# Wo as two partial sums in column mode, a new unit order, and the last rows kept on chip, in a recurrent-memory transformer kernel

## Chip, cores, metric

The kernel runs on one core of a Trainium2 chip. The metric is the device time of one execution in microseconds (us). Every time below comes from runs that the results mark as fast. "Before" is the tuned kernel the change starts from, "after" the changed one. Engines: PE (TensorE matmul), PEld (its weight loads), DVE (VectorE), ACT (ScalarE), POOL (GpSimd), SP (DMA issue).

## The reference, cut to what matters

```python
def _A_ref(x, mem0, Wq, Wk, Wv, Wo, seg_len):      # S=2048, Dm=512, H=32, Dh=128, M=8, seg=32
    mem = mem0
    for s in range(64):                            # strictly one after the other
        h = concat([mem, x[:, 32*s:32*s+32]])      # 8 memory rows + 32 rows
        q, k, v = h @ Wq, h @ Wk, h @ Wv           # 512 -> 32 heads x 128
        p = softmax(mask(q k^T / sqrt(128)))
        o = (p v) @ Wo                             # 4096 -> 512
        mem = o[:, :8]                             # the next segment needs these 8 rows
        outs.append(o[:, 8:])
# B: linear/dot attention over 4 blocks of 512 rows, 32 heads of 16; result = g*a + (1-g)*b
```

Branch A is a chain of 64 segments: the first 8 rows of a segment's Wo result are the memory of the next. Branch B depends on nothing in A, and the kernel uses its pieces to fill waits.

## The kernel before

A segment is a list of *units*. Each engine executes its part of the units in the order of this list. (The code of this section is condensed.)

```python
A_ORDER = """
    bS K0 Q0 K1 Q1 TK0 TQ0 TK1 V0 bP TQ1 bP bT S0 Fc M0 S1 N0 V1 M1 PV0 E0a N1 E0b Ff PV1 W0 E1a E1b bS W1 Fc bS bP WT
    Ff bT Ff""".split()
A_ENG = dict(K0="dve", K1="act", Q0="dve", Q1="act", V0="act", V1="dve", TK0="act", TK1="dve",
             TQ0="dve", TQ1="act", E0a="act", E0b="act", E1a="dve", E1b="act", last=1)
```

K, Q, V are the projections (0 and 1: halves of 16 heads); T their transposes; S scores; M the softmax sums; N the normalising on DVE; PV the product with V; E its evictions from PSUM; W the two halves of Wo; WT the transposition of Wo's result, from which DVE copies the memory rows into `hT` for the next segment. bS, bP, bT are scores, product and late pieces of branch B. Fc and Ff take the next *fill* piece: a projection pass for the next group of four segments (or a left-over Wo pass) for Fc, and a transposing piece or a piece of a finished group's output ("tail") for Ff. "Left rows" in the text are the last 8 rows of each segment, which a group projects together.

Projections, scores, sums and Wo run in *column mode*: the array is used as four tiles of 128 rows by 32 columns, `128*32` in the timelines below. Transposes and the B product are `128*128` there, PV and the B scores `32*128`.

```python
def wo(b):                      # 2 x 16 matmuls of 512 columns
    ...
    for i in range(4):
        for j in range(4):
            h = 16 * b + 4 * j + i
            pe.matmul(pb[bk][32*j:32*(j+1), :], OT_sb[:, h, 0:32], Wo_sb[:, h, :], ...)
    ...
    if b == 1:                  # high part on ACT, the rest on DVE, each in two pieces of 256 columns
        for k in range(2): evac("act", aW_sb[:, 0, cs], pb[bk][:, cs], ...)
        for k in range(2): dve.tensor_tensor(aW_sb[:, 1, cs], pb[bk][:, cs], aW_sb[:, 0, cs], subtract)

def w_t():                      # 8 matmuls in 128x128 mode: transpose and add the four row groups
    for k2 in range(2):
        for c in (2 * k2, 2 * k2 + 1):
            for k in range(2):
                pe.matmul(pb[bk][:, 32*c:32*(c+1)], aW_sb[:, k, 128*c:128*(c+1)], selL[:, :], ...)
    ...  # DVE: copy the memory rows to hT, the others to aT_st
```

At the end, groups 14 and 15 were finished one after the other, after the last segment, and their rows made a trip through HBM:

```python
for _, u in rest: u()
...
while tails < ngrp or late:
    next_tail(ngrp)
    late.pop(0)[1]()
```

The softmax here doesn't subtract the row's maximum and nothing guards it: scores larger than these inputs give would overflow.

Of the kernel before, what the change touches and what calls it, by code (L numbers as in the profile page):

```python
# [223 lines left out]
def build(nc, es, A_x, A_mem0, A_Wq, A_Wk, A_Wv, A_Wo, B_wq, B_wk, B_wv, B_wo, B_beta, gate_w, out, dbg=None):  # L224
# [31 lines left out]
    def alloc(stack, *specs):  # L256
        for name, shape, dt, n in specs:
# [8 lines left out]
          ("selL", [128, SEG], BF16, 0), ("onesb", [128, 128], BF16, 0), ("mneg", [128, 4, 224], BF16, 0),  # L266
# [18 lines left out]
          ("OT_sb", [128, H, L], BF16, 0), ("OTL", [128, H, SEG], BF16, 2), ("aW_sb", [128, 2, 512], BF16, 0),  # L285
# [82 lines left out]
def plan_const(v):  # L368
# [3 lines left out]
    ident, onesb, mneg, selL = v.ident, v.onesb, v.mneg, v.selL  # L372
# [24 lines left out]
    def late():  # L397
        rl, rob, rmk = Rs("selL"), Rs("onesb"), Rs("mneg")
        gp(lambda g: g.memset(selL[:], 0.0), rl, "selL0", True)
        gp(lambda g: g.memset(onesb[:], 0.0), rob, "onesb0", True)  # L400
# [239 lines left out]
class BAttn:  # L640
# [167 lines left out]
    def finish(self, sb, f):  # L808
# [3 lines left out]
        def ft(pe):  # L812
            ins = None
            for q in range(4):
# [11 lines left out]
    bS K0 Q0 K1 Q1 TK0 TQ0 TK1 V0 bP TQ1 bP bT S0 Fc M0 S1 N0 V1 M1 PV0 E0a N1 E0b Ff PV1 W0 E1a E1b bS W1 Fc bS bP WT  # L826
    Ff bT Ff""".split()
A_ENG = dict(K0="dve", K1="act", Q0="dve", Q1="act", V0="act", V1="dve", TK0="act", TK1="dve",
             TQ0="dve", TQ1="act", E0a="act", E0b="act", E1a="dve", E1b="act", last=1)


def plan_a(v, nseg):
# [10 lines left out]
    OT_sb, OTL, aW_sb, t1_sb, aT_st, selL, g_sb, omg_sb, out2d, g_out = (  # L843
        v.OT_sb, v.OTL, v.aW_sb, v.t1_sb, v.aT_st, v.selL, v.g_sb, v.omg_sb, v.out2d, v.g_out)
# [58 lines left out]
    def ol_units(g):  # L903
# [28 lines left out]
        def ut():  # L932
# [14 lines left out]
            B.give(bk)  # L947
            P.dma(P.group("as%d" % g, "as%d" % par), lambda sp: sp.dma_start(v.aTd[g], aT_st[par][:, :, :]),
# [4 lines left out]
    def tail_units(g):  # L953

        sb, q = g // 4, g % 4
        P.dma(P.group("og%d" % g, "og"), lambda sp: sp.dma_start(oTg[:, :, :], v.oTd[sb, :, :, 128 * q:128 * (q + 1)]),
              reads=[Rs("oTd%d_%d" % (sb, f)) for f in range(4)], writes=[Rs("oTg")], name="ldo%d" % g, scratch=True)
        P.dma(P.group("al%d" % g, "al"), lambda sp: sp.dma_start(aTg[:, :, :], v.aTd[g]), reads=[Rs("aTd%d" % g)], writes=[Rs("aTg")],
              name="lda%d" % g, scratch=True)
# [16 lines left out]
        def uf():  # L976
            bk = B.take()

            def f_atr(pe):
                ins = None  # L980
                for c in range(C):
                    ins = pe.transpose(pb16[bk][:, c * 128:(c + 1) * 128], aTg[:, c, :], ident[:, :])
                return ins
            P.op("pe", f_atr, reads=[Rs("aTg"), Rs("ident")], writes=[rbank[bk]], name="atr%d" % g)
# [11 lines left out]
    def segment(s, fill):  # L996
# [111 lines left out]
        def wo(b):  # L1108
            if b == 0:
                wb["bk"] = B.take()  # L1110
            bk = wb["bk"]

            def f(pe):
                ins = None
                for i in range(4):
                    for j in range(4):
                        h = 16 * b + 4 * j + i
                        ins = pe.matmul(pb[bk][SEG * j:SEG * (j + 1), :], OT_sb[:, h, 0:SEG], Wo_sb[:, h, :],  # L1118
                                        start=(b == 0 and i == 0), stop=(b == 1 and i == 3))
                return ins  # L1120
            P.op("pe", f, reads=[Rs("OT%d_%d" % (b, half)) for half in range(2)] + [Rs("Wo")], writes=[rbank[bk]], name="wo%d_%d" % (s, b))
            if b == 1:
                for k in range(2):
                    cs = slice(256 * k, 256 * (k + 1))
                    evac("act", aW_sb[:, 0, cs], pb[bk][:, cs], [bk], [Rs("aWh%d" % k)], "hi%d_%d" % (s, k))
                for k in range(2):
                    cs = slice(256 * k, 256 * (k + 1))
                    P.op("dve", lambda d, cs=cs: d.tensor_tensor(aW_sb[:, 1, cs], pb[bk][:, cs], aW_sb[:, 0, cs], ALU.subtract),  # L1128
                         reads=[rbank[bk], Rs("aWh%d" % k)], writes=[Rs("aWl%d" % k)], name="lo%d_%d" % (s, k))
                B.give(bk)  # L1130

        def w_t():
            bk = B.take()
            for k2 in range(2):
                def f(pe, k2=k2):
                    ins = None
                    for c in (2 * k2, 2 * k2 + 1):
                        for k in range(2):
                            ins = pe.matmul(pb[bk][:, SEG * c:SEG * (c + 1)], aW_sb[:, k, 128 * c:128 * (c + 1)], selL[:, :],  # L1139
                                            start=(k == 0), stop=(k == 1))  # L1140
                    return ins
                P.op("pe", f, reads=[Rs("aWh%d" % k2), Rs("aWl%d" % k2), Rs("selL")], writes=[rbank[bk]], name="aT%d_%d" % (s, k2))
            asrc = pb[bk][:, 0:128].rearrange("p (j t) -> p j t", t=SEG)
            if s + 1 < nseg:
                P.op("dve", lambda d: d.tensor_copy(hT[(s + 1) % 2][:, :, 0:M], asrc[:, :, 0:M]),  # L1145
                     reads=[rbank[bk]], writes=[Rs("hTm%d" % ((s + 1) % 2))], name="hm%d" % (s + 1))
            P.op("dve", lambda d: d.tensor_copy(aT_st[par][:, :, SEG * r:SEG * (r + 1) - M], asrc[:, :, M:SEG]),
# [51 lines left out]
    late, rest, tails = [], [], 0  # L1199

    def next_tail(done):

        nonlocal tails
        if tails < done and bat.jobs_done >= 4 * (tails // 4) + 4 and not late:
            late.extend(tail_units(tails))
            tails += 1
    for g in range(ngrp):
        fill = (left_units(g + 1) if g + 1 < ngrp else []) + rest
        for r in range(4):
            s = 4 * g + r  # L1210
            if s < nseg:
                next_tail(g - 1)
# [4 lines left out]
    for _, u in rest:  # L1217
        u()
    if nseg == 64:
# [6 lines left out]
        while tails < ngrp or late:  # L1226
# [35 lines left out]
```

## Time and profile before

| before | us |
|---|---|
| time, median of 3 (range) | 1118.8 (1115.9 to 1122.4) |
| profiled execution | 1122.7, span 1121.0 |
| start of segment 1 | 111.5 |
| segments 1 to 57, each (mean) | 15.81 |
| from the last WT to the end | 20.6 |

First, the page: busy time of the engines, and the chain that ended last by engine.

```profile
PE 1006.3 (90%) x24389; PEld 547.4 (49%) x24389; DVE 511.8 (46%) x1309; ACT 670.3 (60%) x1371; POOL 212.2 (19%) x544
PE 76%; ACT 9%; DVE 8%; DMA 3%; issue 3%; SPq 0%; POOL 0%; ACTq 0%; DVEq 0%; POOLq 0%
```

PE, with 76% of the chain, is the engine to look at; a faster ACT or DVE (9% and 8% of it) can help here only where PE waits for it. Next, the list of waits of PE (who waited for whom: total us, times, longest).

```profile
PE ps L1081 <- DVE Pn_sb L1071: 40.9, 46, 1.1
PE ps L967 <- DMA oTg<-scr_oTd: 8.3, 2, 4.3
PE ps L1139 <- DVE aW_sb L1128: 7.3, 12, 1.4
PE ps L939 <- DVE hT L1145: 6.7, 15, 0.7
PE ps L967 <- DVE V_sb L321: 5.5, 13, 0.5
```

L1081 is the second PV waiting for the normalised P, L1139 is WT waiting for the subtraction, L939 the transposition of left-over Wo rows, L967 the tail's B matmul. The wait of 9.0 us for the first left rows (startup) is left out. Now the PE timeline of one segment, from M1 to the next segment's first projection (start, length, engine, line, operation, what, shapes, count, idle before).

```profile
510.40 0.28 PE L1056 MATMUL ps<-P_sb,onesb 128*32 128x160 bf16 x8
510.61 0.27 PE L1081 MATMUL ps<-Pn_sb,V_sb 32*128 32x40 bf16 x16
...
511.91 0.28 PE L1081 MATMUL ps<-Pn_sb,V_sb 32*128 32x40 bf16 x16 [0.93 <-DVE Pn_sb L1071]
...
512.21 1.05 PE L1118 MATMUL ps<-Wo_sb,OT_sb 128*32 128x512 bf16 x16
513.19 0.39 PE L708 MATMUL ps<-QTj,KTj 32*128 32x256 bf16 x4
513.51 1.05 PE L1118 MATMUL ps<-Wo_sb,OT_sb 128*32 128x512 bf16 x16
514.38 1.04 PE L858 MATMUL ps<-Wv_sb,xL 128*32 128x512 bf16 x16
...
515.67 0.36 PE L755 MATMUL ps<-Vj,PT 128*128 128x17 bf16 x8
515.97 0.58 PE L1139 MATMUL ps<-selL,aW_sb 128*128 128x32 bf16 x8
516.40 0.28 PE L783 MATMUL ps<-MZj,pQj 128*128 128x68 bf16 x4
```

How to read it: the ends of pipelined matmuls are modelled and lengths overlap, so compare *starts*. Wo's second half starts at 513.51 and the next pass at 514.38: 0.87 us for 16 matmuls. WT starts at 515.97 and what follows at 516.40: 0.43. Where the array mode changes there is about 0.1 us more (512.21 to 513.19 is 0.98 for the same 16 matmuls). There is 0.93 us of nothing ahead of the second PV, and nothing at all between Wo and WT: the fill pass (514.38), B's scores and B's product cover eviction and subtraction. The last is the PE timeline of the end.

```profile
1100.34 0.58 PE L1139 MATMUL ps<-selL,aW_sb 128*128 128x32 bf16 x8 [1.37 <-DVE aW_sb L1128]
1100.85 1.91 PE L921 MATMUL ps<-Wo_sb,OTL 128*32 128x512 bf16 x32
...
1108.90 1.89 PE L967 MATMUL ps<-woB_sb,oTg 128*128 128x512 bf16 x4 [4.27 <-DMA oTg<-scr_oTd]
...
1115.27 1.89 PE L967 MATMUL ps<-woB_sb,oTg 128*128 128x512 bf16 x4 [4.06 <-DMA oTg<-scr_oTd]
```

Two tails in a row, each with over 4 us for its load, and their 4 matmuls at half clock (the clock record has 0.5 from 1106.4 to the end).

### The profile page before, as it was taken

To read this page: it belongs to the slowest core of one execution; us is meant where nothing else is said; L and a number is where in the kernel's file an instruction comes from. 1 tells how busy PE (TensorE), PEld (TensorE's weight loads), DVE (VectorE), ACT (ScalarE), POOL (GpSimd) and SP (SyncE) were. 2 spreads that over 40 slices of the span, in tenths; PEclk is the share of its full clock that TensorE was granted. 3 is DMA by queue.
4 is the path that set the end of the run, shared out by engine and by line. 5 is a ranking of instruction groups with operands and counts; after the bars stand their busy time and mean duration, and the time that the engine had idled before them with its cause. 6 is when DMAs were issued, how large, how long until landed. Compare 5 with 4: busy or idle time off the path is not lost.

```text
span 1121.0 us, 54313 instructions
## 1 busy us (share of the span) xinstructions
PE 1006.3 (90%) x24389; PEld 547.4 (49%) x24389; DVE 511.8 (46%) x1309; ACT 670.3 (60%) x1371; POOL 212.2 (19%) x544
## 2 busy tenths in 40 slices
PE   8968989999999999999999999999999999999874
PEld 4423545455554555454455554555455555454432
DVE  4743444444445444444454545444444545444331
ACT  4434666666666666666566666666666666655432
POOL 6100121211122121221221222211221122120000
PEclk9988999999999999999999999999999999999997
DMA  8895000000011010000111010000101010000001
GB/s 283 276 323 187 11 15 10 20 11 15 18 27 46 24 28 23 18 18 14 32 32 33 18 32 18 15 21 18 41 23 28 23 27 24 4 15 15 27 3 34
DMA packets 66176, 51.80 MB, mean 46 GB/s; under 512 B 34320, under 2 KB 64408, under 8 KB 64408
## 3 DMA queue, kind: packets, MB, share of 16 engines
q1 hardware_dynamic: 65944, 48.33, 14.7%
q8 instruction: 192, 3.15, 1.2%
q14 instruction: 40, 0.33, 0.1%
HBM read 33.60 MB, written 14.70 MB: 43 GB/s over the span
## 4 chain that ended last, share of the span: by engine, by line
PE 76%; ACT 9%; DVE 8%; DMA 3%; issue 3%; SPq 0%; POOL 0%; ACTq 0%; DVEq 0%; POOLq 0%
PE ps L858 37%; PE ps L1118 10%; PE ps L867 6%; PE ps L708 4%; ACT PT L716 3%; PE ps L755 3%; PE ps L584 2%; DVE Pn_sb L1067 2%; PE ps L921 2%; PE ps L967 2%; PE ps L1081 2%; PE ps L559 1%; PE ps L1139 1%; DMA scr_pQd<-stgp 1%; ACT R_sb L1060 1%
## 5 line engine op out<-in xcount | busy, mean ns | idle before, releaser
L716 ACT ACTIVATE PT<-ps 128x1024 bf16<-128x1024 f32 x160 | 163.1, 1022 | 59.7 <-PE ps L708 55.0
L1118 PE MATMUL ps<-Wo_sb,OT_sb 128*32 128x512 bf16 x2048 | 137.3, 391 | 3.3 <-DMA Wo_sb<-in_A_Wo_dram 3.3
L858 PE MATMUL ps<-Wv_sb,hT 128*32 128x512 bf16 x2048 | 134.6, 381 | 1.6 <-DVE amem L804 0.9
L858 PE MATMUL ps<-Wk_sb,hT 128*32 128x512 bf16 x2048 | 134.3, 382 | 0.8 <-DVE hT L1145 0.6
L724 POOL TENSOR_SCALAR_AFFINE_SELECT PT<-PT 128x256 bf16<-128x256 bf16 (+1 forms) x224 | 98.3, 439 | 191.6 <-ACT PT L716 182.6
L858 PE MATMUL ps<-Wq_sb,hT 128*32 128x512 bf16 x2048 | 133.6, 381 | 0.0
L1172 POOL COPY OTL<-OT_sb 128x256 bf16<-128x256 bf16 x64 | 25.4, 397 | 514.6 <-DVE OT_sb L321 394.0
L1128 DVE TENSOR_TENSOR aW_sb<-ps,aW_sb 128x256 bf16<-128x256 f32 x128 | 48.3, 419 | 157.2 <-ACT aW_sb L319 157.2
L319 ACT ACTIVATE KN_sb<-ps 128x512 bf16<-128x512 f32 x64 | 38.2, 597 | 117.2 <-PE ps L858 117.2
L319 ACT ACTIVATE OT_sb<-ps 128x320 bf16<-128x320 f32 x192 | 75.7, 428 | 19.2 <-PE ps L1090 18.9
L858 PEld LDWEIGHTS ps<-Wq_sb,hT 128*32 128x32 bf16 x2048 | 55.2, 97 | 56.1 <-issue 1.1
L1060 ACT ACTIVATE R_sb<-ps 128x160 f32<-128x160 f32 x128 | 38.8, 303 | 65.5 <-PE ps L1056 65.5
L858 PEld LDWEIGHTS ps<-Wk_sb,hT 128*32 128x32 bf16 x2048 | 49.2, 97 | 56.6 <-issue 7.1
L1081 PE MATMUL ps<-Pn_sb,V_sb 32*128 32x40 bf16 x2048 | 35.5, 178 | 44.2 <-DVE Pn_sb L1071 40.9
L321 DVE COPY QT_sb<-ps 128x512 bf16<-128x512 bf16 x64 | 27.2, 424 | 95.6 <-PE ps L867 95.6
L1118 PEld LDWEIGHTS ps<-Wo_sb,OT_sb 128*32 128x32 bf16 x2048 | 43.9, 97 | 49.7 <-issue 18.5
L321 DVE CAST KN_sb<-ps 128x512 bf16<-128x512 f32 x64 | 44.1, 689 | 51.4 <-PE ps L858 51.3
L1067 DVE TENSOR_TENSOR Pn_sb<-P_sb,R_sb 128x160 bf16<-128x160 bf16 x128 | 44.1, 344 | 47.7 <-ACT R_sb L1063 39.0
L755 PEld LDWEIGHTS ps<-Vj,PT 128*128 128x128 bf16 x1280 | 44.4, 96 | 41.7 <-issue 28.4
L708 PE MATMUL ps<-QTj,KTj 32*128 32x384 bf16 (+3 forms) x512 | 62.9, 303 | 1.1 <-ACT PT L716 0.2
L319 ACT ACTIVATE V_sb<-ps 128x512 bf16<-128x512 f32 x64 | 38.2, 597 | 42.8 <-PE ps L858 42.8
L858 PEld LDWEIGHTS ps<-Wv_sb,hT 128*32 128x32 bf16 x2048 | 46.0, 95 | 34.7 <-ACT R_sb L1060 1.5
(136 smaller groups left out, 1832.6 us busy)
## 6 DMA issues: line engine op xcount, KB each, us to landing
Wk_sb<-in_A_Wk_dram SPq DMA_DIRECT2D x4, 1024.0 KB, 7.3
Wq_sb<-in_A_Wq_dram SPq DMA_DIRECT2D x4, 1024.0 KB, 8.5
Wv_sb<-in_A_Wv_dram SPq DMA_DIRECT2D x4, 1024.0 KB, 7.9
Wo_sb<-in_A_Wo_dram SPq DMA_DIRECT2D x4, 1024.0 KB, 10.7
scr_vd<-V SPq DMA_DIRECT2D x16, 136.0 KB, 5.1
Vj<-scr_vd SPq DMA_DIRECT2D x32, 68.0 KB, 2.5
Wo_sb<-in_A_x_dram SPq DMA_DIRECT2D x4, 512.0 KB, 7.8
scr_kTd<-stgk SPq DMA_DIRECT2D x16, 128.0 KB, 6.1
```

What stands on the lines that cost most here:

```text
L319: P.op("act", lambda a: a.activation(dst, src, ACT.Copy), reads=[v.rbank[k] for k in bks], writes=dres, name=name)
L321: P.op("dve", lambda d: d.tensor_copy(dst, src), reads=[v.rbank[k] for k in bks], writes=dres, name=name)
L708: ins = pe.matmul(v.pb[bks[x]][:, o:o + w], KT[e][r, 128 * kc:128 * (kc + 1)], QT[r, q0:q0 + w], start=True, stop=True, tile_position=(r.s ...
L716: P.op("act", lambda a: a.activation(pt[:, :, :], v.ps[:, bks[0]:bks[1] + 1, :], ACT.Exp, scale=v.SCALE_B), reads=[v.rbank[b] for b in bks ...
L724: P.op("gp", lambda g, mv=mv: g.affine_select(mv, mv, [[0, mv.shape[1]], [1, 128]], ALU.is_ge, 0.0, base=0, channel_multiplier=-1), reads= ...
L755: ins = pe.matmul(v.pb[ob][:, o:o + 17], pt[:, x, col:col + 128], V[:, kc, 17 * h:17 * (h + 1)], start=first, stop=True, skip_group_check= ...
L858: ins = pe.matmul(pb[bk][SEG * j:SEG * (j + 1), :], lhs(c), w_sb[:, c, n0:n0 + 512], start=(c == 0), stop=(c == C - 1))
L867: ins = pe.transpose(pb16[bk][:, i * 128:(i + 1) * 128], nat[:, b, i * 128:(i + 1) * 128], ident[:, :])
L1060: P.op("act", lambda a: a.activation(R_sb[:, b, :], pb[bk][:, 224:384], ACT.Ln), reads=[rbank[bk]], writes=[Rs("R%d" % b)], name="ln%d_%d" ...
L1067: P.op("dve", lambda d: d.tensor_tensor(wide(Pn_sb, b)[:, :, 0:L], wide(P_sb, b)[:, :, 0:L], R_sb[:, b, :].rearrange("p (i q) -> p i q", q ...
L1081: ins = pe.matmul(pb[bks[j]][:, L * i:L * (i + 1)], V_sb[SEG * j:SEG * (j + 1), b, i * E:(i + 1) * E], Pn_sb[SEG * j:SEG * (j + 1), b, LW ...
L1118: ins = pe.matmul(pb[bk][SEG * j:SEG * (j + 1), :], OT_sb[:, h, 0:SEG], Wo_sb[:, h, :], start=(b == 0 and i == 0), stop=(b == 1 and i == 3))
```

## The change

Its intent: make the chain Wo, eviction, subtraction, transposition, memory shorter by halving the width of what has to be evicted; move work into the 0.93 us hole; take the end off HBM. Three parts, cut to their core:

```diff
 # 1. "split": Wo as 64 matmuls of 256 columns; result is 256 columns wide
-                for i in range(4):
-                    for j in range(4):
-                        h = 16 * b + 4 * j + i
-                        ins = pe.matmul(pb[bk][SEG * j:SEG * (j + 1), :], OT_sb[:, h, 0:SEG], Wo_sb[:, h, :], ...)
+                for n in range(0, 16, 2):
+                    for e in range(2):
+                        h = 16 * b + n + e
+                        for d in range(2):
+                            t = SEG * (2 * e + d)
+                            ins = pe.matmul(pb[bk][t:t + SEG, 0:256], OT_sb[:, h, 0:SEG], Wo_sb[:, h, 256 * d:256 * (d + 1)], ...)
...
+                evac("act", aW_sb[:, 0, :], pb[bk][:, 0:256], [bk], [Rs("aWh")], "hi%d" % s)
+                P.op("dve", lambda d: d.tensor_tensor(aW_sb[:, 1, :], pb[bk][:, 0:256], aW_sb[:, 0, :], ALU.subtract), ...)
...
     # WT: 16 matmuls in column mode, selW adds two partial sums
+                for k in range(2):
+                    for c2 in range(2):
+                        for j in range(4):
+                            o = 128 * c2 + SEG * j
+                            ins = pe.matmul(pb[bk][SEG * j:SEG * (j + 1), 64 * c2:64 * (c2 + 1)], aW_sb[:, k, o:o + SEG], selW[:, :], ...)
 # 2. "order"
-    bS K0 Q0 K1 Q1 TK0 TQ0 TK1 V0 bP TQ1 bP bT S0 Fc M0 S1 N0 V1 M1 PV0 E0a N1 E0b Ff PV1 W0 E1a E1b bS W1 Fc bS bP WT
-    Ff bT Ff
+    bS K0 Q0 K1 Q1 TQ0 bT bP bP TK1 TK0 TQ1 V0 S0 V1 M0 S1 N0 Fc M1 PV0 E0b E0a N1 Fc PV1 E1b E1a W0 bS bT W1 Ff bS Ff
+    WT bP Ff
+  (and other engines for the evictions: all four E on ACT, V0 and V1 on DVE, ...)
 # 3. "tail": a group may be finished as soon as its rows are stored; the last group's rows stay in aT_st
-                next_tail(g - 1)
+                next_tail(1)
...
+        next_tail(0)            # last group: load and B matmul first
+        late.pop(0)[1]()
+    for _, u in rest: u()       # then its left-over Wo pass
+    for _, u in late: u()       # then transposes from aT_st, without HBM
```

More of the change, by code (lines that the diff above doesn't have):

```diff
@@ L265, in build @@
           ("gB_sb", [128, HB], F32, 0), ("omgB_sb", [128, HB], F32, 0),
-          ("selL", [128, SEG], BF16, 0), ("onesb", [128, 128], BF16, 0), ("mneg", [128, 4, 224], BF16, 0),
+          ("selL", [128, SEG], BF16, 0), ("selW", [128, 2 * SEG], BF16, 0), ("onesb", [128, 128], BF16, 0), ("mneg", [128, 4, 224], BF16, 0),
           ("pQj", [128, 512], BF16, 0), ("MZj", [128, 136], BF16, 0), ("PT", [128, 2, 512], BF16, 2), ("orow", [128, 4, 128], BF16, 0),
@@ L284, in build @@
           ("P_sb", [128, 2, 224], BF16, 0), ("Pn_sb", [128, 2, 224], BF16, 0), ("R_sb", [128, 2, 160], F32, 0),
-          ("OT_sb", [128, H, L], BF16, 0), ("OTL", [128, H, SEG], BF16, 2), ("aW_sb", [128, 2, 512], BF16, 0),
+          ("OT_sb", [128, H, L], BF16, 0), ("OTL", [128, H, SEG], BF16, 2), ("aW_sb", [128, 2, 256], BF16, 0),
           ("t1_sb", [128, DM], F32, 0), ("aT_st", [128, C, 128], BF16, 2))
@@ L371, in plan_const @@
     M, SEG, L = v.M, v.SEG, v.L
-    ident, onesb, mneg, selL = v.ident, v.onesb, v.mneg, v.selL
+    ident, onesb, mneg, selL, selW = v.ident, v.onesb, v.mneg, v.selL, v.selW
     NEG = -1.0e9
@@ L397, in late @@
     def late():
-        rl, rob, rmk = Rs("selL"), Rs("onesb"), Rs("mneg")
+        rl, rw, rob, rmk = Rs("selL"), Rs("selW"), Rs("onesb"), Rs("mneg")
         gp(lambda g: g.memset(selL[:], 0.0), rl, "selL0", True)
+        gp(lambda g: g.memset(selW[:], 0.0), rw, "selW0", True)
+        for j in range(2):
+            sel(selW[64 * j:64 * j + 64, :], [[-1, 64]], ALU.not_equal, 1.0, 0, 1, rw, "selW1_%d" % j)
         gp(lambda g: g.memset(onesb[:], 0.0), rob, "onesb0", True)
@@ L825 @@
 A_ORDER = """
-    bS K0 Q0 K1 Q1 TK0 TQ0 TK1 V0 bP TQ1 bP bT S0 Fc M0 S1 N0 V1 M1 PV0 E0a N1 E0b Ff PV1 W0 E1a E1b bS W1 Fc bS bP WT
-    Ff bT Ff""".split()
-A_ENG = dict(K0="dve", K1="act", Q0="dve", Q1="act", V0="act", V1="dve", TK0="act", TK1="dve",
-             TQ0="dve", TQ1="act", E0a="act", E0b="act", E1a="dve", E1b="act", last=1)
+    bS K0 Q0 K1 Q1 TQ0 bT bP bP TK1 TK0 TQ1 V0 S0 V1 M0 S1 N0 Fc M1 PV0 E0b E0a N1 Fc PV1 E1b E1a W0 bS bT W1 Ff bS Ff
+    WT bP Ff""".split()
+A_ENG = dict(K0="dve", K1="act", Q0="act", Q1="act", V0="dve", V1="dve", TK0="dve", TK1="act",
+             TQ0="act", TQ1="act", E0a="act", E0b="act", E1a="act", E1b="act", last=0)
 def plan_a(v, nseg):
@@ L842, in plan_a @@
         v.KN_sb, v.QN_sb, v.LN_sb, v.KT_sb, v.QT_sb, v.KTL, v.QTL, v.V_sb, v.VL, v.P_sb, v.Pn_sb, v.R_sb)
-    OT_sb, OTL, aW_sb, t1_sb, aT_st, selL, g_sb, omg_sb, out2d, g_out = (
-        v.OT_sb, v.OTL, v.aW_sb, v.t1_sb, v.aT_st, v.selL, v.g_sb, v.omg_sb, v.out2d, v.g_out)
+    OT_sb, OTL, aW_sb, t1_sb, aT_st, selL, selW, g_sb, omg_sb, out2d, g_out = (
+        v.OT_sb, v.OTL, v.aW_sb, v.t1_sb, v.aT_st, v.selL, v.selW, v.g_sb, v.omg_sb, v.out2d, v.g_out)
     bat, oTg, aTg = v.bat, v.oTg, v.aTg
@@ L947, in ut @@
             B.give(bk)
+            stored.append(g)
+            if g == ngrp - 1:
+                return
             P.dma(P.group("as%d" % g, "as%d" % par), lambda sp: sp.dma_start(v.aTd[g], aT_st[par][:, :, :]),
@@ L953, in tail_units @@
     def tail_units(g):
+        last = g == ngrp - 1
+        rows = aT_st[g % 2] if last else aTg
+        rr = [Rs("aTl%d" % (g % 2))] + [Rs("aTx%d_%d" % (g % 2, r)) for r in range(4)] if last else [Rs("aTg")]
         sb, q = g // 4, g % 4
@@ L957, in tail_units @@
               reads=[Rs("oTd%d_%d" % (sb, f)) for f in range(4)], writes=[Rs("oTg")], name="ldo%d" % g, scratch=True)
-        P.dma(P.group("al%d" % g, "al"), lambda sp: sp.dma_start(aTg[:, :, :], v.aTd[g]), reads=[Rs("aTd%d" % g)], writes=[Rs("aTg")],
-              name="lda%d" % g, scratch=True)
+        if not last:
+            P.dma(P.group("al%d" % g, "al"), lambda sp: sp.dma_start(aTg[:, :, :], v.aTd[g]), reads=[Rs("aTd%d" % g)], writes=[Rs("aTg")],
+                  name="lda%d" % g, scratch=True)
         def ub():
@@ L981, in f_atr @@
                 for c in range(C):
-                    ins = pe.transpose(pb16[bk][:, c * 128:(c + 1) * 128], aTg[:, c, :], ident[:, :])
+                    ins = pe.transpose(pb16[bk][:, c * 128:(c + 1) * 128], rows[:, c, :], ident[:, :])
                 return ins
-            P.op("pe", f_atr, reads=[Rs("aTg"), Rs("ident")], writes=[rbank[bk]], name="atr%d" % g)
+            P.op("pe", f_atr, reads=rr + [Rs("ident")], writes=[rbank[bk]], name="atr%d" % g)
             P.op("dve", lambda dv: dv.scalar_tensor_tensor(fin, pb16[bk][:, 0:512], g_sb[:, g:g + 1], t1_sb[:, :],
@@ L1114, in f @@
                 ins = None
-                for i in range(4):
-                    for j in range(4):
-                        h = 16 * b + 4 * j + i
-                        ins = pe.matmul(pb[bk][SEG * j:SEG * (j + 1), :], OT_sb[:, h, 0:SEG], Wo_sb[:, h, :],
-                                        start=(b == 0 and i == 0), stop=(b == 1 and i == 3))
+                for n in range(0, 16, 2):
[3 more added lines that the diff above has]
+                            t = SEG * (2 * e + d)
+                            ins = pe.matmul(pb[bk][t:t + SEG, 0:256], OT_sb[:, h, 0:SEG], Wo_sb[:, h, 256 * d:256 * (d + 1)],
+                                            start=(b == 0 and n == 0), stop=(b == 1 and n == 14))
                 return ins
@@ L1122, in wo @@
             if b == 1:
-                for k in range(2):
-                    cs = slice(256 * k, 256 * (k + 1))
-                    evac("act", aW_sb[:, 0, cs], pb[bk][:, cs], [bk], [Rs("aWh%d" % k)], "hi%d_%d" % (s, k))
-                for k in range(2):
-                    cs = slice(256 * k, 256 * (k + 1))
-                    P.op("dve", lambda d, cs=cs: d.tensor_tensor(aW_sb[:, 1, cs], pb[bk][:, cs], aW_sb[:, 0, cs], ALU.subtract),
-                         reads=[rbank[bk], Rs("aWh%d" % k)], writes=[Rs("aWl%d" % k)], name="lo%d_%d" % (s, k))
+                evac("act", aW_sb[:, 0, :], pb[bk][:, 0:256], [bk], [Rs("aWh")], "hi%d" % s)
+                P.op("dve", lambda d: d.tensor_tensor(aW_sb[:, 1, :], pb[bk][:, 0:256], aW_sb[:, 0, :], ALU.subtract),
+                     reads=[rbank[bk], Rs("aWh")], writes=[Rs("aWl")], name="lo%d" % s)
                 B.give(bk)
@@ L1133, in w_t, with f @@
             bk = B.take()
-            for k2 in range(2):
-                def f(pe, k2=k2):
-                    ins = None
-                    for c in (2 * k2, 2 * k2 + 1):
-                        for k in range(2):
-                            ins = pe.matmul(pb[bk][:, SEG * c:SEG * (c + 1)], aW_sb[:, k, 128 * c:128 * (c + 1)], selL[:, :],
-                                            start=(k == 0), stop=(k == 1))
-                    return ins
-                P.op("pe", f, reads=[Rs("aWh%d" % k2), Rs("aWl%d" % k2), Rs("selL")], writes=[rbank[bk]], name="aT%d_%d" % (s, k2))
-            asrc = pb[bk][:, 0:128].rearrange("p (j t) -> p j t", t=SEG)
+            def f(pe):
+                ins = None
+                for k in range(2):
+                    for c2 in range(2):
+                        for j in range(4):
+                            o = 128 * c2 + SEG * j
+                            ins = pe.matmul(pb[bk][SEG * j:SEG * (j + 1), 64 * c2:64 * (c2 + 1)], aW_sb[:, k, o:o + SEG], selW[:, :],
+                                            start=(k == 0 and c2 == 0), stop=(k == 1), skip_group_check=True)
+                return ins
+            P.op("pe", f, reads=[Rs("aWh"), Rs("aWl"), Rs("selW")], writes=[rbank[bk]], name="aT%d" % s)
+            src = pb[bk][:, 0:128].rearrange("p (e d t) -> p d e t", e=2, d=2)
             if s + 1 < nseg:
-                P.op("dve", lambda d: d.tensor_copy(hT[(s + 1) % 2][:, :, 0:M], asrc[:, :, 0:M]),
+                P.op("dve", lambda d: d.tensor_copy(
+                    hT[(s + 1) % 2][:, :, 0:M].rearrange("p (d e) t -> p d e t", d=2), src[:, :, :, 0:M]),
                      reads=[rbank[bk]], writes=[Rs("hTm%d" % ((s + 1) % 2))], name="hm%d" % (s + 1))
-            P.op("dve", lambda d: d.tensor_copy(aT_st[par][:, :, SEG * r:SEG * (r + 1) - M], asrc[:, :, M:SEG]),
+            P.op("dve", lambda d: d.tensor_copy(
+                aT_st[par][:, :, SEG * r:SEG * (r + 1) - M].rearrange("p (d e) t -> p d e t", d=2), src[:, :, :, M:SEG]),
                  reads=[rbank[bk]], writes=[Rs("aTx%d_%d" % (par, r))], name="atx%d" % s)
@@ L1198, in plan_a, with next_tail @@
         u()
-    late, rest, tails = [], [], 0
-    def next_tail(done):
+    late, rest, stored, tails = [], [], [], 0
+    def next_tail(least):
         nonlocal tails
-        if tails < done and bat.jobs_done >= 4 * (tails // 4) + 4 and not late:
+        if tails < ngrp and len(stored) >= tails + least and bat.jobs_done >= 4 * (tails // 4) + 4 and not late:
             late.extend(tail_units(tails))
             tails += 1
+            return True
     for g in range(ngrp):
@@ L1216, in plan_a @@
         rest = ol_units(g)
-    for _, u in rest:
-        u()
     if nseg == 64:
@@ L1225, in plan_a @@
         bat.run_late()
-        while tails < ngrp or late:
-            next_tail(ngrp)
+        while tails < ngrp - 1 or late:
+            next_tail(1)
             late.pop(0)[1]()
+        next_tail(0)
+        late.pop(0)[1]()
+    for _, u in rest:
+        u()
+    for _, u in late:
+        u()
 _INS = ['A_x', 'A_mem0', 'A_Wq', 'A_Wk', 'A_Wv', 'A_Wo', 'A_seg_len', 'B_x', 'B_wq', 'B_wk', 'B_wv', 'B_wo', 'B_beta', 'gate_w']
```

## The prediction

> **What bounds the kernel now.** TensorE. The page's first part has PE busy 90% (ACT 60, DVE 46); the chain of waits is 76% PE. The timeline repeats a segment of 15.0 us (Wk starts at 502.05, 517.04); the mean of segments 1 to 57 is 15.8. What is idle (list of waits, PE): PV of the second half waits for the normalised P 46 times, 40.9 us (0.93 each); the transposition of Wo's result waits for the subtraction, 7.3; transposes of the left rows 6.7; the tail's B matmul 8.3 for its DMA and 5.5 for a PSUM copy.
>
> **Costs, from the timeline (start to start).** A column-mode pass of 16 matmuls of 512 columns takes 0.87 us. Wo as 32 of 256 streams as many columns. Weight loads are no limit: score matmuls of 40 columns follow each other 16 in 0.11 us. So no gain there. The transposition (8 matmuls, 128x128 mode) takes 0.43; as 16 column-mode matmuls of 64 columns I estimate 0.12. A change of array mode costs about 0.1 (Wk to Wq 0.87, last Wq to transposes 0.97). [...] The new order has about 13 changes a segment for 12. Net PE work: about -0.2 us a segment, -13 in all. B's late pieces between Wo's halves add two changes each: +4.
>
> **Waits.** A fill pass (0.87+0.1) now stands between the two PVs and covers the 0.93 wait. It came from after the second Wo half, where it covered eviction and subtraction. That chain shrinks (two 0.35-0.43 us evictions to one, two subtractions to one) but is still: last matmul +1.1 us from the Wo start, eviction 0.43, subtraction 0.42, about 0.1 to PE: 2.2 us. PE has 0.87 + a B score pair 0.4. So the wait moves: I expect 0.85 us before the transposition where nothing fills, about 0.4 where a transposing fill does, none under a tail's matmul: 25-30 us in all. Perhaps 0.1-0.2 a segment stays at the second PV (10). Other segment waits mostly go. Net: -25.
>
> **Tail.** From the last transposition (1100.3) to the end are 20.7 us, with two serial tails of 6.4, each with a DMA wait of over 4, at half clock. Now tail 14 falls into segments, the last B matmul runs without waiting and the last rows need no trip through HBM: about 11 us remain, -9.
>
> **Sum.** -13 +4 +2 -25 -9 = -41 us: 1078 us, 8 in 10 between 1058 and 1099. Chances: faster by over 2% 0.85, within 2% 0.13, slower 0.02.
>
> **Right or wrong.** PV's wait for normalised P should fall from 41 to under 12 us; the wait of the transposition for the subtraction rise from 7 to 20-35; a Wo pass stay 0.87-0.90 start to start; the transposition take under 0.2; the stretch after the last one shrink to 10-12 us.
>
> **What would make it wrong.** Wo at 256 columns exposing weight loads (0.2 a pass would cost 26 us); a longer wait at the transposition, as the eviction queues behind B's 1.02 us exponential on ACT; the second Wo half or PV waiting for ACT, which now takes all four PV evictions; more half-clock stretches (two in mid-run before, each 3.4 us at clock 0.5, costing 1.7[...]).

Two passages that stated hardware behaviour without a measurement of this case are cut from this text; no term of the sum is, and it still comes to -41 us. Three of its numbers can be followed here. The 0.12 us for the new transposition is an estimate; the 0.87 us of 16 matmuls of 512 columns give 0.11 us in proportion for 16 of 64. The mode changes, counted in the traces between segments 1 and 57, are 12.2 a segment before and 14.0 after. And the eviction of 256 columns takes 0.38 us in both traces (mean; 0.43 is that of PV's 320 columns); the chain that was put at 2.2 us takes 2.16 from the second Wo half to the transposition where nothing fills.

## The result

| | before | after |
|---|---|---|
| median us (range) | 1118.5 (1115.9 to 1122.4), 4 runs | 1084.4 (1082.3 to 1087.6), 4 runs |
| profiled span | 1121.0 | 1082.3 |
| start of segment 1 | 111.5 | 113.0 |
| segments 1 to 57 | 885.6 | 856.9 |
| segment 57 to last WT | 103.3 | 103.7 |
| last WT to end | 20.6 | 8.7 |

The ratio is 0.9695 (95% interval 0.966 to 0.973). Ratios here are the mean time of one kernel's fast runs over that of the other's in the same rounds, so not quite the ratio of the medians. The gain lies in two places: 28.7 us in the 56 segments and 11.9 us at the end. (These are of the two profiled executions, whose spans differ by 38.6 us; the medians differ by 34.) The same views of the profile after, first the page and the waits of PE:

```profile
PE 988.9 (91%) x26927; PEld 593.2 (55%) x26949; DVE 437.4 (40%) x1117; ACT 703.7 (65%) x1435; POOL 212.8 (20%) x547
PE 76%; ACT 10%; DVE 7%; issue 3%; DMA 2%; SPq 0%; POOL 0%; ACTq 0%; DVEq 0%; POOLq 0%
```

```profile
PE ps L1151 <- DVE aW_sb L1137: 19.3, 27, 1.1
PE ps L861 <- DVE LN_sb L321: 10.3, 25, 0.5
...
PE ps L861 <- DVE V_sb L321: 6.4, 12, 0.6
PE ps L861 <- DVE VL L321: 5.3, 14, 0.4
PE ps L1151 <- ACT QTL L319: 4.2, 13, 0.5
PE ps L1091 <- DVE Pn_sb L1081: 3.7, 4, 0.9
```

PE still makes up 76% of the chain. The wait of the second PV (L1091) has fallen from 40.9 to 3.7 us, and WT (L1151) waits 25 us in three lines (two shown: 19.3 and 4.2). Waits at L861 are new: the left passes (for LN_sb and VL, 15.6 us), and the second pass of V, which waits for the eviction of the first (V_sb, 6.4 us). The timeline of a segment shows both.

```profile
502.39 0.27 PE L1091 MATMUL ps<-Pn_sb,V_sb 32*128 32x40 bf16 x16
...
503.14 1.05 PE L861 MATMUL ps<-Wv_sb,xL 128*32 128x512 bf16 x16 [0.39 <-DVE VL L321]
504.12 0.27 PE L1091 MATMUL ps<-Pn_sb,V_sb 32*128 32x40 bf16 x16
...
504.41 1.06 PE L1131 MATMUL ps<-Wo_sb,OT_sb 128*32 128x256 bf16 x32
505.40 0.39 PE L711 MATMUL ps<-QTj,KTj 32*128 32x256 bf16 x4
505.72 1.06 PE L1131 MATMUL ps<-Wo_sb,OT_sb 128*32 128x256 bf16 x32
506.71 0.39 PE L711 MATMUL ps<-QTj,KTj 32*128 32x512 bf16 x2
507.88 0.30 PE L1151 MATMUL ps<-selW,aW_sb 128*32 128x64 bf16 x16 [0.78 <-DVE aW_sb L1137]
508.11 0.36 PE L758 MATMUL ps<-Vj,PT 128*128 128x17 bf16 x8
```

Wo with 32 matmuls of 256 columns takes 0.99 us from start to start (504.41 to 505.40) with its mode change, as 16 of 512 did (0.98). WT takes 0.23 to the next start, of which about 0.1 is the change to 128x128 mode. The fill pass at 503.14 now stands between the PVs, but it waits for the eviction of the pass before it (VL by DVE), because the allocator gives it the same PSUM bank (in other_bank, below, it gets another one, and such waits fall from 15.6 to 1.9 us). The end:

```profile
1073.59 0.30 PE L1151 MATMUL ps<-selW,aW_sb 128*32 128x64 bf16 x16 [1.10 <-DVE aW_sb L1137]
1074.05 0.81 PE L977 MATMUL ps<-woB_sb,oTg 128*128 128x512 bf16 x3 [0.16 <-issue]
1074.79 1.91 PE L924 MATMUL ps<-Wo_sb,OTL 128*32 128x512 bf16 x32
1078.94 0.40 PE L992 MATMUL ps<-ident,aT_st 128*128 128x128 bf16 x4 [0.37 <-ACT aT_st L946]
```

No load is waited for (one matmul of the four at 1074.05 is missing from the trace).

To see where a segment's time goes, the starts in the PE timeline are averaged over segments 1 to 56 (all in us). Wk is the first projection pass of a segment, T its first transposition, PV0 and PV1 are the two PVs, W1 is the second half of Wo. A half-clock stretch is a time in which the trace's clock record shows PE at 0.5 of its clock; "half" is the number of them between segments 1 and 57, each of 3.4 us:

| | Wk to T | T to PV0 | PV0 to PV1 | PV1 to W1 | W1 to WT | WT to next Wk | sum | half |
|---|---|---|---|---|---|---|---|---|
| before | 3.57 | 5.37 | 1.39 | 1.63 | 2.46 | 1.39 | 15.81 | 2 |
| after | 3.57 | 5.11 | 1.70 | 1.72 | 2.29 | 0.92 | 15.30 | 1 |
| only_split | 3.57 | 5.36 | 1.39 | 1.67 | 2.51 | 1.30 | 15.80 | 1 |
| only_order | 3.89 | 5.12 | 1.68 | 1.70 | 2.48 | 1.09 | 15.95 | 11 |
| no_split | 3.74 | 5.12 | 1.68 | 1.70 | 2.48 | 1.08 | 15.79 | 6 |
| only_tail | 3.57 | 5.36 | 1.38 | 1.62 | 2.42 | 1.39 | 15.74 | 0 |
| evict_twice | 3.68 | 5.11 | 1.71 | 1.70 | 2.62 | 0.93 | 15.74 | 4 |
| fill_back | 3.73 | 5.12 | 1.35 | 1.75 | 3.42 | 0.91 | 16.27 | 9 |
| after_again | 3.57 | 5.11 | 1.73 | 1.73 | 2.28 | 0.93 | 15.35 | 1 |
| other_bank | 3.60 | 5.11 | 1.44 | 1.80 | 2.35 | 0.92 | 15.21 | 2 |
| late_B_after | 3.76 | 5.11 | 1.71 | 1.64 | 2.34 | 1.24 | 15.79 | 7 |
| full_mode_T | 3.57 | 5.14 | 1.67 | 1.76 | 2.28 | 0.79 | 15.21 | 1 |
| banks_full_T | 3.60 | 5.25 | 1.43 | 1.79 | 2.36 | 0.79 | 15.21 | 2 |
| banks_full_T_bP | 3.57 | 5.25 | 1.42 | 1.76 | 2.44 | 0.64 | 15.08 | 0 |

### The profile page after: what moved, and what is told of

The parts are those of the page before. It is cut to its first block, busy times and chain, and to the rows that moved or that the text cites. A ratio compares the mean times of both kernels' runs of the same rounds, so it can differ in the third digit from the quotient of the medians.

```text
span 1082.3 us, 59045 instructions
## 1 busy us (share of the span) xinstructions
PE 988.9 (91%) x26927; PEld 593.2 (55%) x26949; DVE 437.4 (40%) x1117; ACT 703.7 (65%) x1435; POOL 212.8 (20%) x547
## 4 chain that ended last, share of the span: by engine, by line
PE 76%; ACT 10%; DVE 7%; issue 3%; DMA 2%; SPq 0%; POOL 0%; ACTq 0%; DVEq 0%; POOLq 0%
PE ps L861 37%; PE ps L1131 9%; PE ps L870 6%; PE ps L711 3%; PE ps L758 3%; ACT PT L719 3%; PE ps L587 2%; PE ps L562 2%; PE ps L924 2%; ACT aW_sb L319 2%; PE ps L1151 2%; DVE LN_sb L321 2%; PE ps L1091 1%; ACT R_sb L1070 1%; ACT R_sb L1073 1%
## 5 line engine op out<-in xcount | busy, mean ns | idle before, releaser
L1131 PE MATMUL ps<-Wo_sb,OT_sb 128*32 128x256 bf16 x4096 | 140.2, 279 | 3.4 <-DMA Wo_sb<-in_A_Wo_dram 1.7
L861 PE MATMUL ps<-Wv_sb,hT 128*32 128x512 bf16 x2048 | 134.7, 381 | 6.4 <-DVE V_sb L321 6.4
L861 PE MATMUL ps<-Wk_sb,hT 128*32 128x512 bf16 x2048 | 133.3, 380 | 3.4 <-DVE hT L1157 3.4
L861 PE MATMUL ps<-Wq_sb,hT 128*32 128x512 bf16 x2048 | 132.7, 379 | 0.0
L319 ACT ACTIVATE QN_sb<-ps 128x512 bf16<-128x512 f32 x128 | 76.5, 597 | 79.7 <-PE ps L861 79.7
L727 POOL TENSOR_SCALAR_AFFINE_SELECT PT<-PT 128x256 bf16<-128x256 bf16 (+1 forms) x224 | 98.3, 439 | 140.2 <-ACT PT L719 117.2
L321 DVE CAST V_sb<-ps 128x512 bf16<-128x512 f32 x128 | 88.6, 692 | 88.5 <-PE ps L861 66.4
L1131 PEld LDWEIGHTS ps<-Wo_sb,OT_sb 128*32 128x32 bf16 x4096 | 99.6, 98 | 20.4 <-ACT OT_sb L319 8.2
L319 ACT ACTIVATE OT_sb<-ps 128x320 bf16<-128x320 f32 x256 | 96.7, 431 | 4.5 <-PE ps L1100 4.3
L1137 DVE TENSOR_TENSOR aW_sb<-ps,aW_sb 128x256 bf16<-128x256 f32 x64 | 27.2, 425 | 154.5 <-ACT aW_sb L319 154.4
L861 PEld LDWEIGHTS ps<-Wq_sb,hT 128*32 128x32 bf16 x2048 | 54.8, 97 | 55.7
L321 DVE COPY KT_sb<-ps 128x512 bf16<-128x512 bf16 x64 | 27.1, 423 | 133.8 <-PE ps L870 133.8
L861 PEld LDWEIGHTS ps<-Wk_sb,hT 128*32 128x32 bf16 x2048 | 48.8, 96 | 58.5 <-DVE aT_st L1160 8.7
L319 ACT ACTIVATE QT_sb<-ps 128x512 bf16<-128x512 bf16 x128 | 76.9, 601 | 0.0
L1049 ACT ACTIVATE P_sb<-ps 128x224 bf16<-128x224 f32 x128 | 44.6, 349 | 44.4 <-PE ps L1043 44.4
L861 PEld LDWEIGHTS ps<-Wv_sb,hT 128*32 128x32 bf16 x2048 | 46.0, 95 | 39.6 <-DVE V_sb L321 7.5
L1077 DVE TENSOR_TENSOR Pn_sb<-P_sb,R_sb 128x160 bf16<-128x160 bf16 x128 | 41.7, 325 | 26.7 <-ACT R_sb L1073 16.3
```

The source lines that it names most:

```text
L319: P.op("act", lambda a: a.activation(dst, src, ACT.Copy), reads=[v.rbank[k] for k in bks], writes=dres, name=name)
L321: P.op("dve", lambda d: d.tensor_copy(dst, src), reads=[v.rbank[k] for k in bks], writes=dres, name=name)
L727: P.op("gp", lambda g, mv=mv: g.affine_select(mv, mv, [[0, mv.shape[1]], [1, 128]], ALU.is_ge, 0.0, base=0, channel_multiplier=-1), reads= ...
L861: ins = pe.matmul(pb[bk][SEG * j:SEG * (j + 1), :], lhs(c), w_sb[:, c, n0:n0 + 512], start=(c == 0), stop=(c == C - 1))
L1049: P.op("act", lambda a: a.activation(P_sb[:, b, :], pb[bk][:, 0:224], ACT.Exp, scale=SCALE), reads=[rbank[bk]], writes=[Rs("P%d" % b)], na ...
L1077: P.op("dve", lambda d: d.tensor_tensor(wide(Pn_sb, b)[:, :, 0:L], wide(P_sb, b)[:, :, 0:L], R_sb[:, b, :].rearrange("p (i q) -> p i q", q ...
```

## Experiments

All twelve runs gave correct results. First the change was taken apart.

### The parts alone

`only_split`: before plus part 1. `only_order`: before plus part 2. `only_tail`: before plus part 3. `no_split`: after minus part 1.

```diff
 # no_split, against after
-   (part 1: wo, w_t and aW_sb of 256 columns)
+   (wo, w_t and aW_sb of before)
```

> Only the two partial sums of 256 columns and their column-mode transposition; order and end as before. Theory (parts help each other): in the old order the transposition stands between two groups of 128x128-mode work, so it pays two mode changes (0.2 us) for 0.3 us saved, and its wait for the subtraction (7.3 us) goes: 8 to 12 us faster than before, 1107 to 1111. Rival (parts are independent, split is worth its 0.3 us of PE a segment plus the shorter eviction wherever it stands): 18 to 20 us faster.

> Only the new order of units and the new engines; Wo 512 columns wide, end as before. Theory: the second PV's wait for normalised P falls from 41 to under 8 us, but the transposition now waits about 0.4 us longer in each unfilled segment than with the split (two evictions and two subtractions), 40 to 50 us in all: 0 to 8 us faster than before. Rival (independent): the order is the main gain by itself, 12 us or more faster.

> Only the last group's rows kept in SBUF and tail 14 moved into the segments; Wo and order as before. Both theories: 8 to 11 us faster than before; the stretch from the last transposition to the end 9 to 12 us instead of 20.7.

> The changed kernel with Wo 512 columns wide and the old transposition. Theory (parts help each other): the split is worth more in the new order than in the old one, 16 to 24 us; so 10 to 18 us faster than before. Rival (independent): it equals only_order plus only_tail and the split is worth the same here as in only_split, within 3 us.

| | median us | ratio to before (95%) | against before |
|---|---|---|---|
| only_split | 1119.1 | 1.000 (0.997 to 1.003) | nothing |
| only_order | 1130.0 | 1.010 (1.007 to 1.014) | 1% slower |
| only_tail | 1107.4 | 0.990 (0.987 to 0.993) | 1% faster |
| no_split | 1118.7 | 0.999 (0.995 to 1.004) | nothing |
| after (all three) | 1084.4 | 0.970 (0.966 to 0.973) | 3% faster |

The tail is worth what was expected, 10 us, and stands by itself. The other two parts are not independent at all: the split alone gives nothing, the order alone costs 1%, and together (without the tail) they give 2%. Put the other way, the split is worth 0 in the old order and 34 us in the new (no_split to after). My expectation had only this interplay right: I had expected gains of 8 to 12 us from the split alone, 0 to 8 from the order alone and 10 to 18 in no_split, and all three missed. Half of the rival held: no_split is what only_order and only_tail give together (1.010 x 0.990 = 1.000, measured 0.999). Its other half, a split worth the same everywhere, failed.

*Why the split alone gives nothing.* In the old order WT hardly waited (7.3 us; 4.2 in only_split), since the fill pass covered the chain. So a shorter chain had nothing to shorten: W1 to WT even rose from 2.46 to 2.51, because WT in column mode now follows B's product, which is in 128x128 mode (the trace has 14.0 mode changes a segment instead of 12.2). WT to the next Wk fell by only 0.09: the transposition of left-over rows that follows waits longer (11.5 instead of 6.7 us in the list of waits).

*Why the order alone loses.* From before to only_order the columns of the table other than Wk to T fall by 0.18 us together (10.3 us over the 56 segments). Wk to T rises by 0.324, 18.1 us, with 11 half-clock stretches instead of 2. So the order saves time in itself, and loses more than that to the clock.

*Why the order needs the split.* From no_split to after the 56 segments get 27.2 us shorter (884.1 to 856.9). The table says where: W1 to WT 0.184 x 56 = 10.3 us (the chain), WT to Wk 0.161 x 56 = 9.0 (the transposition itself), and Wk to T 0.175 x 56 = 9.8, with -1.9 elsewhere. (The profiled execution of no_split was its fastest, 1111.7 us, so this is less than the 34 us of the medians.) The last was not in my sum. It is not work: the projections are the same. The PE timeline of no_split shows it.

```profile
640.68 0.59 PE L1149 MATMUL ps<-selL,aW_sb 128*128 128x32 bf16 x8 [1.05 <-DVE aW_sb L1138]
...
641.72 1.25 PE L861 MATMUL ps<-Wk_sb,hT 128*32 128x512 bf16 x16
642.74 1.93 PE L861 MATMUL ps<-Wq_sb,hT 128*32 128x512 bf16 x16
644.45 1.73 PE L861 MATMUL ps<-Wk_sb,hT 128*32 128x512 bf16 x16
```

After a wait of 1.05 us ahead of WT, the projection pass that starts at 642.74 takes 1.71 us instead of 0.87: half the clock for 3.4 us, a loss of 1.7 us (Wk to T is 5.0 to 5.26 in such segments of no_split instead of 3.57). The clock record of this trace shows the stretch as 3.413 us at 0.5. Waits of about a microsecond came before it: each of the 17 half-clock stretches of no_split and only_order follows a 3.4 us window with just one PE wait of over 0.1 us in it, the one ahead of WT, of 0.75 to 1.38 us. In no_split and only_order 43 segments have the same unfilled W1 to WT of about 2.42 us, and 6 and 11 stretches at half clock lie between segments 1 and 57; in after the unfilled ones have 2.16 us, and there is 1 stretch. The mean clock of all four executions of each kernel says the same: 0.964 to 0.972 in only_order, 0.971 to 0.977 in no_split, 0.987 to 0.989 in after (0.980 to 0.993 in its six later executions).

Why do equal waits cost the clock only in some segments? The traces tell much of it. In each of the 14 traces all half-clock stretches start on one grid of 3.413 us. Cut the time from segment 1 to 57 into the windows of that grid, leave out those at half clock, and add up PE's busy time in each (with its modelled ends). Of the 31 windows with PE busy for less than 60%, 28 were followed by a half-clock stretch; of the 49 with 60 to 68%, 15; of the 3441 above that, 4. Windows under 68% occur 10 times in no_split, 13 times in only_order and once in after. So it looks as if the idle time within one window of the grid counts, and the wait ahead of WT matters by where it falls on the grid. This is a correlation read from the traces; no run shifted the grid against the segments.

### The chain made long again

To tell the chain from everything else in the split, `evict_twice` keeps after's matmuls and only repeats the eviction.

```diff
-                evac("act", aW_sb[:, 0, :], pb[bk][:, 0:256], [bk], [Rs("aWh")], "hi%d" % s)
+                for again in range(2):
+                    evac("act", aW_sb[:, 0, :], pb[bk][:, 0:256], [bk], [Rs("aWh")], "hi%d_%d" % (s, again))
```

> The changed kernel with the eviction of Wo's result (0.38 us on ACT) done twice before the subtraction, so that the chain behind Wo is as long as it was with 512 columns while all PE work stays. Theory (what the split pays for in this order is this chain, and a wait that gets longer also drops PE to half clock more often): second Wo half to transposition grows from 2.29 by 0.25 to 0.33 us, and half-clock stretches between segments 1 and 57 rise from 1 to between 4 and 9, seen as Wk to transposes above 3.65 instead of 3.57: 18 to 28 us slower than the changed kernel. Rival (half-clock stretches come by chance, not from the longer wait): 12 to 17 us slower with 0 to 2 stretches.

Measured: 1113.2 us, ratio to before 0.994 (0.992 to 0.997) where after has 0.967 to 0.970; that is about 29 us slower than after, a little more than expected. W1 to WT rose by 0.325 (18.2 us over 56 segments), Wk to T by 0.115 (6.4 us, 4 half-clock stretches). So 0.38 us more on ACT, with PE work untouched, undoes most of the gain: in this order the chain after Wo is on the critical path. That the longer wait also brings the clock down fits (13 windows under 68% busy instead of 1), but is shown less firmly: it is 4 stretches against 1 in one trace each, and the clocks of the four executions (0.978 to 0.988) overlap those of after. The chain was also made longer than with 512 columns, 2.57 us from W1 to WT where nothing fills against 2.42 in no_split, and still there were fewer stretches than there (4 against 6); the length of the wait alone does not set their number.

### The fill pass back behind Wo

```diff
-    ... PV0 E0b E0a N1 Fc PV1 E1b E1a W0 bS bT W1 Ff bS Ff
+    ... PV0 E0b E0a N1 PV1 E1b E1a W0 bS bT W1 Fc Ff bS Ff
```

> The changed kernel with the second fill pass put back behind the second Wo half, where the old order had it. Theory (the place between the two PVs is only slightly better than the old one, since the pass costs two mode changes and a bank wait there and leaves a wait behind Wo): PV0 to PV1 falls from 1.70 to about 1.40, second Wo half to transposition rises from 2.29 to about 2.85, 5 to 13 us slower than the changed kernel. Rival (it saves the whole 0.93 us wait, some 40 us): 25 us or more slower.

Measured: 1148.6 us, 1.025 (1.021 to 1.028) of before, 64 us slower than after. Both expectations failed in size, and the experiment turned out to test something else too, as its waits of PE show.

```profile
PE ps L1091 <- DVE Pn_sb L1081: 48.0, 53, 0.9
PE ps L942 <- DVE LN_sb L930: 24.3, 16, 1.6
PE ps L870 <- ACT LN_sb L319: 12.8, 32, 0.5
```

The PV wait is back (48.0). But in three of four segments of a group, the Ff that follows is the transposition of the very pass that Fc has just made (L942, L870), and PE waits for its eviction: 37 us. In the fourth kind of segment, where Fc makes V of the left rows, which need no transposition, fill_back is *faster* than after by 0.40 us a segment (mean of 14). So it is not shown that the place between the PVs is better for covering waits; what is shown is that the new order puts 2 to 3 us between a fill pass and the piece that consumes it, and that a fill pass must not stand just ahead of its consumer.

### Three possible improvements

These ran together with after itself (`after_again`), on one chip, five rounds.

```diff
 # other_bank: second pass of each pair of left passes takes one of the two "long" banks (0 and 1, which other takes use last)
-                    bk = B.take()
+                    bk = B.take(long=b == 1)
 # late_B_after
-    ... W0 bS bT W1 Ff bS Ff WT bP Ff
+    ... W0 bS W1 bT Ff bS Ff WT bP Ff
 # full_mode_T: the same sums with 4 matmuls in 128x128 mode
-                        for j in range(4):
-                            o = 128 * c2 + SEG * j
-                            ins = pe.matmul(pb[bk][SEG * j:SEG * (j + 1), 64 * c2:64 * (c2 + 1)], aW_sb[:, k, o:o + SEG], selW[:, :], ...)
+                        ins = pe.matmul(pb[bk][:, 64 * c2:64 * (c2 + 1)], aW_sb[:, k, 128 * c2:128 * (c2 + 1)], selW[:, :], ...)
```

> The changed kernel once more, unaltered, so that the three others can be held against it on the same chip: 1082 to 1088 us, 3.0% faster than before (plus or minus 0.4).

> The changed kernel; only the second pass of each pair of left-row passes takes its PSUM bank from the two that the first pass has not just used. Theory (the fill between the two PVs waits for the first fill's eviction because the allocator hands it the same bank; PE's waits of 15 us on the left passes): those waits go to under 3 us, PV0 to PV1 falls from 1.70 to about 1.35 us on average, and the kernel gets 12 to 18 us faster than the changed one. Rival (the wait is really the slow DVE chain, and would show at the second PV instead): the second PV's wait for normalised P grows by as much and the time stays within 3 us.

> The changed kernel; B's late piece (128x128 mode) moved from between the two Wo halves to behind the second one. Theory (a mode change costs about 0.1 us, and the piece would fill part of the wait before the transposition): first Wo half to second falls from 1.415 to 1.31 us, second half to transposition does not grow by more than 0.03; 5 to 9 us faster than the changed kernel. Rival (mode changes are not what the extra 0.1 us is): within 2 us.

> The changed kernel; the transposition as 4 matmuls in 128x128 mode (128 weight columns, 64 moving) instead of 8 x 2 in column mode; the same sums. Theory (what pays is the halved width, not column mode: 4 matmuls at 0.054 us are 0.22 us, and the B matmuls that follow need no mode change): within 3 us of the changed kernel. Rival (column mode by itself saves 0.2 to 0.3 us a segment): 8 us or more slower.

| | median us | ratio to before (95%) |
|---|---|---|
| after_again | 1083.3 | 0.967 (0.964 to 0.971) |
| other_bank | 1079.2 | 0.962 (0.961 to 0.964) |
| late_B_after | 1108.6 | 0.992 (0.988 to 0.995) |
| full_mode_T | 1078.6 | 0.962 (0.960 to 0.964) |

*full_mode_T.* Expected: within 3 us. Measured: about 6 us faster (the ratio of the two ratios is 0.994), because WT to the next Wk fell by 0.13: B's product, which follows, is in 128x128 mode too, so a mode change goes (the trace has 12.7 a segment instead of 14.0). WT takes 0.11 us to the next start instead of 0.23. So column mode was not what made the transposition cheap: at the halved width 4 matmuls in 128x128 mode take 0.11 us, where the 8 of the full width take 0.43 in before. (The 0.054 us a matmul of the expectation is that 0.43 divided by 8; it was twice too high here.) A change of mode costs about 0.1 us here: 0.98 against 0.87 for the same 16 matmuls, and 0.13 for the one that goes.

*other_bank.* The bank wait did go (the left passes' waits for DVE are 1.9 us in the list), and PV0 to PV1 fell by 0.30 us, 16.7 us over the 56 segments. But only some 8 us arrived in these segments, and 4 to 6 in the time. Of the rest, PV1 to W1 took 4.0 us, W1 to WT 3.6 and one more half-clock stretch 1.7. A part was eaten by stalls in the middle of Wo and PV groups that no semaphore explains ("issue"):

```profile
545.40 0.83 PE L1131 MATMUL ps<-Wo_sb,OT_sb 128*32 128x256 bf16 x23
547.33 0.50 PE L1131 MATMUL ps<-Wo_sb,OT_sb 128*32 128x256 bf16 x9 [1.10 <-issue]
```

Between 120 and 1060 us there are 17 gaps of over 0.45 us between the starts of two neighbours of one group of matmuls, 12.1 us in sum; after_again has 12 (8.9 us), before has 4 (3.0 us). All 17 ended 1.2 to 1.7 us after a transfer of 16 KB of kind "instruction" had landed on DMA queue q8; a moment taken at random has such a landing behind it in 11% of cases. It is the same in the other kernels: 4 of 4 in before, 10 of 10 in after, 12 of 12 in after_again, 8 of 10 in only_order. Before has 192 of these blocks and after 211, or 254 and 255 matmuls and weight loads of PE for each block. What holds PE in these stalls is not shown: the traces show that stalls and landings go together, a tight correlation, and no run varied the landings.

*late_B_after.* Expected: 5 to 9 us faster. Measured: 25 to 27 slower. W0 to W1 fell from 1.43 to 1.33 as expected, but WT to the next Wk rose by 0.32 (17.7 us over the 56 segments), and 7 half-clock stretches came up (Wk to T rose by 0.19, 10.7 us). The timeline of DVE and PE in a segment with such a piece:

```profile
428.81 0.42 DVE L1137 TENSOR_TENSOR aW_sb<-ps,aW_sb 128x256 bf16<-128x256 f32 x1 [3.70 <-ACT aW_sb L319]
429.16 0.25 DVE L791 RECIPROCAL rden<-ps 128x16 f32<-128x16 f32 x1
...
429.39 0.36 PE L1151 MATMUL ps<-selW,aW_sb 128*32 128x64 bf16 x16
...
430.81 0.42 DVE L807 TENSOR_TENSOR amem<-ps,rden 128x256 f32<-128x256 f32 x1
...
431.48 0.18 DVE L1157 CAST hT<-ps 128x32 bf16<-128x32 f32 x1
...
431.71 0.61 PE L711 MATMUL ps<-QTj,KTj 32*128 32x384 bf16 x4 [1.68 <-DVE hT L1157]
```

The late piece is not only a PE piece. Its seven small DVE instructions (429.16 to 431.23), which in after stand ahead of the subtraction in DVE's queue, now stand between the subtraction and the copy of the memory rows. WT was issued at 429.39, but the copy came at 431.48. I had looked at the place in PE's queue alone.

### Better versions

`banks_full_T` joins other_bank and full_mode_T, and gives the second V pass a long bank too. `banks_full_T_bP` also has B's product ahead of WT (`Ff bS Ff bP WT Ff`).

> A better version: the changed kernel with the other bank for the second left pass and for the second V pass, and the transposition as 4 matmuls in 128x128 mode. Parts gave 5 to 6 us each: 1070 to 1076 us. If the parts work on the same wait: 1077 to 1080.

> The same with the B product put ahead of the transposition instead of behind it, to fill the wait there. If its mask is ready by then, the wait of the transposition falls by about 0.2 us a segment and 5 to 10 us are gained: 1062 to 1070 us. If its mask (POOL after B's exponential) comes later than the subtraction, it delays the transposition and with it the next segment: 1075 us or more, and PE waits for PT from POOL.

Measured: 1072.9 us (0.958, 0.956 to 0.960) and 1069.2 us (0.955, 0.952 to 0.957). Both beat both kernels; the second is about 1.3% faster than after. Its waits of PE:

```profile
PE ps L758 <- POOL PT L727: 11.3, 23, 0.8
PE ps L1149 <- DVE aW_sb L1137: 5.5, 14, 1.1
```

WT's wait for the subtraction has gone down to 5.5 us (19.3 in after), but B's product now waits 11.3 us for its mask from POOL, as the second half of the expectation feared; W1 to WT rose by 0.09 and WT to Wk fell by 0.15, a net 0.06 a segment. In both versions T to PV0 is 0.14 us longer than in after and 0.11 longer than in full_mode_T, so the long bank for the V pass costs something in these segments, while the stretch from segment 57 to the last WT in the two traces is 98.3 and 100.2 us against 103.7 in after's. A version with that bank only where B has ended was not run.

## Why the prediction was right or wrong

The predicted 1078 us missed the 1084.4 by 0.6%, and the range held. Point by point:

- *PE bounds, Wo at 256 columns costs no more.* Right: 0.99 us with a mode change against 0.98.
- *The second PV's wait falls from 41 to under 12.* Right: 3.7 us.
- *The transposition's wait rises from 7 to 20-35.* Right: 25 us in three lines, 1.0 to 1.1 us where nothing fills (I had 0.85).
- *The transposition takes under 0.2 us.* Not quite: 0.23 to the next start, since the following change of mode has to be paid. From no_split to after, WT to the next Wk fell by 9.0 us over 56 segments, where the predicted 0.2 a segment makes 11.2.
- *Tail -9, 10-12 us remain.* Right in kind, a bit too cautious: 8.7 us remain, -11.9 in the profile, 10 us in only_tail.
- *B's late pieces between Wo's halves: +4.* Right: PV1 to W1 rose by 0.084, 4.7 us over 56 segments. But late_B_after shows that they stand there for DVE's sake.
- *"Perhaps 0.1-0.2 a segment stays at the second PV (10)".* The size was about right and the place was wrong: 15.6 us stay one step earlier, at the fill pass, which gets the PSUM bank of the pass before it.
- *The sum.* That it came so near is partly luck: two of its terms were off in opposite directions. The waits were to fall by 25 us. PE's listed waits between segments 1 and 57 (those over 0.15 us) add up to 55.4 us before and 50.0 after, a fall of 5: what PV0 to PV1 lost (44.1 to 20.0) came back for the most part ahead of WT (2.7 to 23.9). The work was to fall by 7 (-13 +4 +2). What is left of the 28.7 us, some 23, lies there and in pauses too short for the list. Part of it is WT (0.43 to 0.23, 11 us). Another part was in no term of the sum: T to PV0 fell by 0.26 us a segment, 14.6 us, and has two mode changes in the new order instead of four. Nor does the sum say how the gain hangs together: without the split the order is a loss (+1%), without the order the split is nothing. I had listed half-clock stretches as a risk of the change; in the runs they are a cost of the order that the split takes away again (9.8 us of no_split to after).

What stays open: whether the issue stalls come from the instruction blocks that land 1.2 to 1.7 us before their end (seen together in the traces, not varied), and what exactly sets off a half-clock stretch where PE is busy for 60 to 68% of a window, since only 15 of 49 such windows did.

## What to carry to other kernels

A shorter dependent chain paid here only where the order had taken the cover off it (0 us in the old order, 34 in the new), and taking the cover off paid only with the short chain (1% lost without it): test such changes together and apart before you add their gains. Before moving a piece, follow it on every engine's queue and into the PSUM banks it takes; here a piece that looked free on PE cost 25 us by way of DVE's queue and the clock, and a bank choice held up PE for 0.30 us a segment, of which half came through to the time. Waits of about a microsecond that recur can cost more than themselves: in no_split and only_order a 3.4 us window with one wait of 0.75 to 1.38 us came before each of 17 stretches at clock 0.5, each a loss of 1.7 us; look at the clock record, not only at the list of waits.
